# One hand-written instruction order replaced by another in a fused attention and mixture-of-experts kernel

## The chip, the cores and the metric

The kernel runs on one core of one Trainium2 chip. The metric is the device time of one execution in microseconds (us). The engines of the core are named as the profile names them: PE (TensorE matmuls) and PEld (its weight loads), DVE (VectorE), ACT (ScalarE), POOL (GpSimd, which here also issues the casting loads) and SP (SyncE, which issues the other transfers). Every engine works through its own instructions in the order in which the program has them, and waits on semaphores for the others.

## What is computed

Linear attention with phi(x) = elu(x) + 1 over 8 batches, 8 heads, 576 positions and 64 channels; its output, 4608 tokens of width 512, goes into a mixture of 8 experts whose gates are balanced by eight Sinkhorn rounds.

```python
q_p, k_p = (phi(q), phi(k))
kv = np.einsum('bhsd,bhse->bhde', k_p, v)
z = np.sum(k_p, axis=2)
num = np.einsum('bhsd,bhde->bhse', q_p, kv)
den = np.einsum('bhsd,bhd->bhs', q_p, z)[..., None] + 1e-06
x = (num / den)                     # as 4608 x 512
P = np.exp(x @ w_gate - max)        # 4608 x 8
for _ in range(8):
    P /= P.sum(1, keepdims=True) + 1e-09
    P /= P.sum(0, keepdims=True) + 1e-09
    P *= N / E
for e in range(E):
    out += P[:, e:e + 1] * (np.maximum(x @ w1[e], 0.0) @ w2[e])
```

## The kernel before

**Stages.** Attention runs over 16 pairs of heads (`att`, numbered 0 to 15 below as pair n). Of each pair, K, Q and V are loaded; ACT takes an exponential of K and of Q (`f_e`, `f_qe`); DVE makes phi from them (`f_t` and `f_m` for K, `f_qm` and `f_qp` for Q); PE forms the key-value product (`f_kv`, line 411) and transposes phi(Q) (`f_qt`, line 437); copies out of PSUM follow (`f_z` twice, `f_qc`); then PE makes the denominators (`f_den`), ACT their logarithm and reciprocal (`f_ln`, `f_ex`), PE the numerators (`f_num`, line 468), and DVE the quotient into xT (`f_x`, line 496). K of pair 0 is loaded through SP, all the other K, Q, V and all weights through POOL, with a cast on the way for Q, V and the weights; at most eight of POOL's loads are outstanding (`p_sw`). Before there is real work, PE runs up to 46 idle matmuls on a block of zeros (`f_warm`, line 588), which the order places one by one.

The experts run over 9 groups of 512 tokens. Expert 0 begins while attention still runs: a group's first layer (`f_hq`, line 682, and its relu `f_rl`, lines 687 and 689) and second layer (`f_y`, line 930, and its eviction `f_fin`) need only the tokens of that group. From the fifth group on, both layers use a fast matrix scheme with seven products in place of eight (`block7` for the first layer with its products in line 808, `unit` for the second with line 1048). One expert and one group make a unit, numbered 9e + g; from unit 9 on, the repeating pattern, every unit has the same work and its PE order is a fixed chain. A unit needs sums of its hidden layer (`f_S`, line 1019, four a unit). An expert needs, once, four combinations W of its first weights (`f_W`, line 980) and four combinations T of its second weights (`f_T`, line 994), each one DVE instruction with both inputs in SBUF. Results are evicted with their gate into `acc`: most by DVE (line 1079), two a unit by an ACT multiplication (line 1086) and a POOL addition (line 1089). What expert 0 left in `acc` before the gates were known is scaled later, 32 instructions named `f_s`, by ACT or DVE.

**What sets the order.** The class `_Plan` holds 4744 tasks, each with an id, the engines that can do it, a duration, and what it depends on. `run` emits them one at a time. First it takes the tasks of `_FRONT`, a list of ids written out by hand, each with a letter for the engine: p PE, a ACT, d DVE, g POOL, s SP, m a transfer, n nothing. After the list has ended, a greedy rule chooses: the engine that can start earliest, and of its tasks the one of the lowest `prio`. Only the order on each engine, and for tasks that two engines can do the choice of engine, reach the program. The list of before has 1510 entries. It ends in unit 17, the last of expert 1.

Ids that matter below: pair 0 has 50 (load Q), 52 (load V), 54 (`f_e`), 55 (`f_t`), 56 (`f_m`), 58 (`f_kv`), 59 and 60 (`f_z`), 62 to 64 (`f_qe`, `f_qm`, `f_qp`), 65 (`f_qt`), 66 (`f_qc`), 67 (`f_den`); 76 and 78 load K and Q of pair 1, 82 is its `f_e`; 109, 111, 114 and 116 load the quarters of expert 0's first weights; 533 closes the attention; 1535 and 1537 load the first weights of expert 2 and 1541 the second; 1544 to 1547 are the four `f_W` of expert 2, 1548 to 1551 its four `f_T`. An `f_T` may not start before a product of an earlier unit is done, which for 1551 is in unit 17:

```python
tT = add(("dve", 0.685), f_T, deps=tw2 + ([x_closed[0]] if e > 0 else xu[0] + xu[1]) + [tT, pe_id.get((NG * (e - 1) + i + 5, "b22"))], acq=[gT] if i == 0 and e > 0 else [], use=[gw2, gT],
         prio=-900.0 if e > 1 else 5.0)
```

Of the kernel before, what the change touches and what calls it, by code (L numbers as in the profile page):

```python
# [17 lines left out]
class _Plan:  # L18
# [121 lines left out]
    1n 108n 119n 607n 48s 49m 2p 3p 52g 53m 4p 50g 51m 5p 6p 76g 77m 7p 8p 0g 9p 78g 79m 10p 54a 55d 11p 126g 127m  # L140
    12p 13p 14p 15p 80g 81m 16p 56d 17p 18p 128g 129m 19p 20p 21p 57n 22p 130g 131m 23p 24p 25p 154g 155m 26p 27p 28p
    29p 30p 31p 61n 32p 62a 63d 33p 34p 35p 36p 58p 64d 156g 157m 82a 109g 110m 37p 59d 65p 60d 89n 111g 112m 38p 90a
    66d 39p 83d 67p 40p 158g 159m 68a 41p 84d 42p 43p 132a 44p 133d 69p 85n 114g 115m 86p 91d 70a 92d 87a 71a 116g
    117m 139n 93p 141d 45p 94d 88a 140a 182g 183m 72p 46p 73d 95p 96a 134d 74p 184g 185m 160a 97p 75d 135n 142d 98a
    136p 167n 186g 187m 161d 143p 137a 99a 138d 47p 120g 121m 144d 100p 101d 145p 113n 210g 211m 608p 146a 162d 102p
    609p 168a 103d 610p 163n 212g 213m 147p 169d 164p 148a 170d 149a 214g 215m 171p 165d 611p 166d 172a 150p 118n
    240g 241m 612p 151d 614p 613a 616p 615a 152p 242g 243m 618p 153d 173p 620p 189d 123g 124m 195n 188a 174a 622p
    190d 196a 197d 175p 191n 244g 245m 192p 621a 198d 176a 623d 624p 193a 619a 194d 199p 617d 625a 626p 122n 268g
    269m 177a 200d 180p 644n 201p 630p 181d 202a 217d 178p 628p 179d 223n 216a 224a 203p 298g 299m 627d 645p 218d
    270g 271m 204a 647p 225d 219n 205a 226d 328g 329m 220p 646d 106g 107m 648a 227p 247d 221a 649p 222a 228d 253n  # L150
    246a 206p 650d 229p 651p 254a 255d 207d 653p 230a 300g 301m 248d 125n 208p 654a 231p 104g 105m 209d 629p 232a
    256d 249n 272g 273m 233a 250p 636d 652d 257p 251a 252a 631p 275d 258d 632p 305d 259p 236p 638d 655p 281n 274a
    304a 260a 276d 282a 633p 237d 261p 283d 234p 262a 634p 284d 384g 385m 235d 263a 302g 303m 285p 311n 657p 326g
    327m 286d 339n 312a 354g 355m 266p 341d 238p 267d 340a 330g 331m 277n 306d 278p 239a 656a 356g 357m 640d 635p
    279a 342d 358g 359m 280a 658a 313d 287p 264p 314d 288a 659p 307n 265d 642a 289p 677n 290a 308p 333d 332a 660d
    315p 386g 387m 309d 678p 291a 316d 382g 383m 680p 310d 412g 413m 361d 360a 317p 292p 663p 318a 293d 440g 441m
    367n 679a 334d 319p 414g 415m 294p 320a 665p 295d 335n 681a 343p 362d 321a 336p 344d 395n 368a 397d 296p 337d
    369d 338a 568d 666p 297a 396a 389d 322p 345p 323d 682p 442g 443m 346a 370d 673a 324p 416g 417m 684p 325d 363n
    388a 347p 398d 364p 348a 499g 500m 683d 349a 371p 365d 472g 473m 569d 686p 372d 470g 471m 366a 685a 352p 373p
    353d 661p 374a 390d 418a 425n 350p 375p 351d 688p 391n 376a 687d 392p 419d 377a 399p 420d 468g 469m 393a 690p  # L160
    400d 444g 445m 394a 446a 453n 380p 455d 401p 381d 662p 402a 570d 378p 426a 664p 379d 421n 403p 689a 427d 422p
    428d 404a 501g 502m 477s 447d 691a 478s 429p 503g 504m 479s 423a 671d 692p 405a 508s 430d 667p 454a 424d 448d
    431p 406p 432a 668p 407d 669a 433p 509s 516n 456d 710n 408p 434a 711p 409d 449n 693a 457p 675d 510s 511g 435a
    571s 572m 589d 450p 573s 574m 505a 484n 590d 696p 458d 518d 451a 697p 517a 452d 486d 459p 591d 436p 460a 694p
    592s 593m 437d 704a 461p 506d 438p 462a 695p 439d 712a 410p 507d 463a 519d 512n 464p 713p 411a 485a 465d 520p
    475d 466p 521a 700p 467d 715p 487d 702a 474a 561d 488p 562d 513p 714a 476d 701p 489d 514a 480n 515a 563d 522p
    716d 564s 565m 481p 523a 566s 567m 524p 482d 717p 525a 483d 575d 527p 526a 490p 698p 576d 718a 528d 719p 491a
    529p 492p 530d 721p 493a 582d 720a 497p 699p 494a 583d 722d 723p 706a 498d 725p 724a 747d 708a 495p 584d 751n
    752p 726a 496d 585s 586m 587s 588m 754p 748d 559n 577d 531p 790d 755a 578s 579m 580s 581m 848d 727p 532a 753a
    533n 743d 728p 534d 594s 595m 756p 733p 757a 744d 734p 849d 745d 535p 758p 741a 536d 760p 537d 759a 762p 761a  # L170
    764p 763a 735a 766p 791d 596g 765a 597n 603n 792d 746d 729p 793s 794m 850d 560p 749d 851s 852m 730p 853s 854m
    750d 538p 798p 737a 539d 731p 795s 796m 799a 540d 767a 732p 1021s 1022m 804p 1078s 1079m 739a 797n 802p 805a 772p
    803a 768d 812p 769d 773a 808p 813a 770d 541p 800p 774p 771d 801a 542d 818p 809d 814p 819a 543d 778p 815a 776p
    806p 777a 816p 779d 822p 817a 820p 823d 810p 807d 782p 811a 821d 775a 544p 824p 545d 856p 825a 906d 858p 857a
    783d 780p 859a 907d 784p 826d 827d 862p 785a 855n 860p 908d 863a 781d 864p 909s 910m 830p 911s 912m 604g 605m
    598g 599m 600g 601m 546d 832p 831a 861a 870p 836p 871a 865d 876p 837d 872p 877a 547p 874p 828d 873a 880p 548d
    875a 866p 881d 833a 878p 829d 840p 867d 882p 841d 868p 834p 879d 869a 549d 883a 914p 842p 915a 835a 838p 606n
    843a 920p 913n 884d 550p 928p 921a 885d 916p 888p 551d 917a 964d 918p 889a 965d 922p 919a 839d 924p 894p 886d
    929a 923d 890p 602n 925d 930p 887d 934p 931a 966d 932p 895d 935a 967s 968m 926p 969s 970m 552d 933a 892p 927a
    936p 891a 972p 938p 973a 898p 939d 978p 899d 553p 940p 937d 900p 941a 554d 555d 896p 901a 979a 976p 971n 974p  # L180
    982p 975a 986p 977a 980p 942d 946p 987a 893d 983d 992p 990p 943d 993a 988p 947a 897d 996p 989a 984p 944d 952p
    985a 1013d 950p 1014d 953a 991a 1015d 994p 948p 981d 997d 956p 949a 945d 1024p 1016d 954p 1025a 957d 998p 958p
    999a 1534n 1535g 1536m 1026p 1537g 1538m 959a 1012n 1023n 1017d 1030p 1027a 995d 1000p 1031a 955d 556p 1032p 557d
    1001p 558d 1028p 703a 846d 1034p 639d 1002p 1008a 738d 1029a 1035d 1003p 670a 1033d 1036p 1018d 1038p 643d 1004p
    1039a 787d 951a 709d 1040p 1539n 740d 1037a 1044p 1009d 1041a 1005p 674d 1045a 676d 1046p 847a 637d 1042p 904a
    1019d 1006p 1043a 788d 1048p 705d 1081p 1047d 1007p 1049d 1082a 641d 1083p 1080n 1540n 1010d 1050p 1084a 1087p
    1020d 1135s 1136m 1541g 1542m 1051a 1089p 1011d 1088a 1085p 1052d 1056p 1086a 1053d 1058p 1057a 1054d 1061p 1055d
    1059d 1091p 1062a 1060d 1066p 1064a 1063g 1090d 960a 1069p 1092d 672a 1067d 707a 1093p 1068d 1095p 1071d 1097p
    1070d 1096a 1072p 1098a 1094a 1101p 1543n 1074d 1103p 1073d 1102a 1099p 1104d 1105p 1100a 1138p 1106d 1140p 1139a
    1075p 1141a 742a 1107p 1077d 1137n 1144p 1076d 1108a 1192s 1193m 1146p 1109d 1142p 1113p 1110d 1115p 1111d 1114a  # L190
    905d 1145a 1118p 1112d 1116d 1148p 1121a 1117d 1123p 789a 1149d 1122g 1143a 1126p 1065g 1124d 1147d 1150p 1125d
    1152p 1151a 1128d 1154p 1153a 1129p 1155a 1158p 1130d 1160p 1131d 1159a 1156p 1162p 1157a 1195p 1163d 1119a 1197p
    1196a 1120g 962d 1132p 1198a 1161d 1164p 1133d 1194n 1201p 1134d 1165a 1249s 1250m 1203p 844d 736a 1199p 1166d
    1170p 1202a 1127d 1167d 1172p 1171a 1168d 1200a 1175p 1173d 1169d 1205p 1178a 1174d 1180p 1176a 1206d 1183p 1204d
    1181d 1207p 1182d 1209p 1185d 1211p 1210a 1186p 1212a 1208a 1215p 1187d 1217p 1184d 1216a 1213p 1188d 1219p 1214a
    1252p 1220d 1254p 1253a 1218d 1189p 1255a 1221p 1191d 1251n 1258p 1190d 1222a 1306s 1307m 1260p 786a 1223d 1256p
    1227p 1259a 1224d 1257a 1229p 1225d 1228a 1226d 1232p 1261d 1262p 1230d 1233a 1237p 1231d 1234g 1263d 1240p 1179g
# [1009 lines left out]
```

## Time and profile before

| | |
|---|---|
| median of 3 runs | 963.76 us (963.01 to 964.25) |
| the profiled execution | 965.29 us |
| its span, first to last instruction | 963.5 us |
| ACT busy | 579.6 us (60%) |
| POOL busy | 146.1 us (15%) |
| DMA, mean | 117 GB/s |
| granted TensorE clock, mean | 1.000 |

Times inside the profile count from the start of the span; 1.8 us of the profiled execution lie outside it. A table by windows gives, for every stretch, the busy time of each engine with the number of its instructions in brackets. In a timeline each line has the start, the duration, the engine and the instruction, and in square brackets how long the engine had been idle before it and who released it.

### The profile page before, as it was taken

How to read it: one execution, taken by the hardware profiler on the slowest of the kernel's cores; microseconds unless marked ns; L12 is line 12 of the kernel's file. 1: busy time of each engine (PE TensorE's matmuls, PEld its weight loads, DVE VectorE, ACT ScalarE, POOL GpSimd, SP SyncE). 2: the span in 40 equal slices, each digit the busy share in tenths (PEclk: the TensorE clock that was granted, in tenths of full speed). 3: DMA queues.
4: the chain of work that ended last, by engine and by line, in shares of the span. 5: the costliest groups of instructions: out<-in, count | busy, mean ns of one | idle time of the engine just before them, and what ended most of it. 6: DMA issues, size and time to landing. Idle time of an engine off the chain costs nothing.

```text
span 963.5 us, 21102 instructions
## 1 busy us (share of the span) xinstructions
PE 950.4 (99%) x8576; PEld 804.8 (84%) x8576; DVE 784.7 (81%) x1501; ACT 579.6 (60%) x1032; POOL 146.1 (15%) x210
## 2 busy tenths in 40 slices
PE   8999999999999999999999999999999999999998
PEld 4555578788888888888888888888888888888886
DVE  6999999987788888878887888878887888877775
ACT  6999765666655555555555555555555555555552
POOL 6442000010112111111111111111112111111110
PEclk9999999999999999999999999999999999999999
DMA  9998391252227222362227222272226322235654
GB/s 227 267 235 202 136 252 67 44 122 78 78 78 165 78 77 78 101 142 77 78 78 157 86 78 78 73 163 69 70 73 138 97 75 76 78 100 164 165 162 112
DMA packets 45693, 112.52 MB, mean 117 GB/s; under 512 B 4380, under 2 KB 25628, under 8 KB 45596
## 3 DMA queue, kind: packets, MB, share of 16 engines
q1 hardware_dynamic: 21068, 75.57, 23.4%
q0 software_dynamic: 24128, 35.07, 19.2%
q8 instruction: 67, 1.10, 0.4%
q10 hardware_dynamic: 400, 0.52, 0.2%
q14 instruction: 30, 0.25, 0.1%
HBM read 119.69 MB, written 17.69 MB: 143 GB/s over the span
## 4 chain that ended last, share of the span: by engine, by line
PE 89%; DVE 4%; DMA 3%; ACT 2%; issue 1%; SPq 1%; POOL 0%; DVEq 0%; POOLq 0%; ACTq 0%
PE ye L1048 35%; PE hq L808 23%; PE R L808 12%; PE Zye L1048 6%; PE Zye L808 6%; PE ye L930 2%; PE hq L682 2%; DMA xs<-xd 2%; DMA kin<-in_k_dram 1%; PE yw L588 1%; DVE xT L496 1%; PE kv_ps L411 1%; PE att L468 0%; PE num_ps L468 0%; ACT rden L481 0%
## 5 line engine op out<-in xcount | busy, mean ns | idle before, releaser
L1079 DVE SCALAR_TENSOR_TENSOR acc<-ye,P_sb,acc 128x256 f32<-128x256 f32 x620 | 268.1, 479 | 124.5 <-PE ye L1048 123.1
L808 PEld LDWEIGHTS <-W 128*128 128x128 f16 x2144 | 209.8, 98 | 25.3
L1048 PEld LDWEIGHTS <-S 128*128 128x128 f16 x1984 | 194.1, 98 | 23.8 <-DVE S L1019 1.0
L1048 PE MATMUL ye<-T,S 128*128 128x256 f16 x1488 | 192.8, 273 | 0.9 <-DVE S L1019 0.8
L1089 POOL TENSOR_TENSOR acc<-acc,st 128x256 f32<-128x256 f32 x124 | 87.8, 727 | 626.2 <-ACT st L1086 626.2
L808 PEld LDWEIGHTS <-w 128*128 128x128 f16 x1608 | 157.4, 98 | 19.1 <-issue 0.5
L1048 PEld LDWEIGHTS <-h 128*128 128x128 f16 x1584 | 154.9, 98 | 19.4 <-issue 1.4
L843 ACT ACTIVATE h<-hq 128x512 f16<-128x512 f32 x134 | 80.0, 598 | 148.5 <-PE hq L808 145.7
L808 PE MATMUL hq<-xs,W 128*128 128x256 f16 x1008 | 151.2, 273 | 0.0
L808 PE MATMUL R<-xs,W 128*128 128x256 f16 x1008 | 151.2, 273 | 0.0
L808 PE MATMUL hq<-xs,w 128*128 128x256 f16 x1008 | 140.9, 273 | 0.3 <-DVE h L846 0.3
L840 ACT ACTIVATE h<-Zye 128x512 f16<-128x512 f32 x134 | 80.2, 598 | 39.2 <-PE Zye L808 39.2
L1086 ACT ACTIVATE st<-Zye,P_sb 128x256 f32<-128x256 f32 x124 | 52.5, 471 | 76.3 <-PE Zye L1048 75.5
L846 DVE CUSTOM_DVE_ANT_0 h<-R,s 128x512 f16<-128x512 f32 x126 | 86.5, 687 | 9.9 <-ACT s L830 9.9
L1019 DVE TENSOR_TENSOR S<-h 128x1024 f16<-128x1024 f16 x124 | 85.3, 688 | 11.0 <-ACT h L843 11.0
L830 ACT COPY s<-hq 128x512 f32<-128x512 f32 x126 | 73.5, 584 | 34.3 <-PE hq L808 34.2
L823 ACT COPY Zye<-hq 128x512 f32<-128x512 f32 x134 | 77.8, 580 | 21.8 <-PE hq L808 21.7
L846 DVE CUSTOM_DVE_ANT_0 h<-hq,s 128x512 f16<-128x512 f32 x126 | 86.6, 688 | 4.7 <-PE hq L808 4.5
L808 PE MATMUL Zye<-xs,w 128*128 128x256 f16 x504 | 75.6, 273 | 0.0
L837 ACT COPY s<-R 128x512 f32<-128x512 f32 x126 | 74.5, 591 | 0.7 <-PE R L808 0.7
L1048 PE MATMUL ye<-w,h 128*128 128x256 f16 x528 | 68.4, 273 | 1.2 <-DVE acc L1079 1.2
L1048 PE MATMUL Zye<-w,h 128*128 128x256 f16 x528 | 68.4, 273 | 0.0
(117 smaller groups left out, 979.2 us busy)
## 6 DMA issues: line engine op xcount, KB each, us to landing
xs<-xd SPq DMA_DIRECT2D x63, 896.0 KB, 4.5
kin<-in_k_dram POOLq DMA_DIRECT2D x15, 576.0 KB, 8.6
out_dram<-acc SPq DMA_DIRECT2D x67, 128.0 KB, 2.4
w<-in_moe_w_dram POOLq DMA_DIRECT2D x16, 512.0 KB, 9.5
w<-in_moe_w_dram POOLq DMA_DIRECT2D x7, 1024.0 KB, 13.1
vv<-in_v_dram POOLq DMA_DIRECT2D x16, 288.0 KB, 7.6
qin<-in_q_dram POOLq DMA_DIRECT2D x16, 288.0 KB, 9.0
xd<-acc SPq DMA_DIRECT2D x5, 512.0 KB, 2.7
```

The costliest lines, as they stand in the source:

```text
L808: nc.tensor.matmul(dst[:, p, :], lhsT=lhs(p, c), rhs=rhs(c), start=(first and p == 0 and c == 0), stop=(c == 1), skip_group_check=True)
L823: nc.scalar.copy(out=Zt[1], in_=gX["tile"])
L830: nc.scalar.copy(out=gs2["tile"], in_=gX["tile"])
L837: nc.scalar.copy(out=gs5["tile"], in_=gR["tile"])
L840: nc.scalar.activation(out=hd(0, 0), in_=Zt[1], func=AF.Relu)
L843: nc.scalar.activation(out=hd(1, 0), in_=gX["tile"], func=AF.Relu)
L846: nc.vector._custom_dve(TENSOR_ADD_SAT, out=dst, in0=ps, in1=sb, s0=3.0e38, s1=0.0)
L1019: nc.vector.tensor_tensor(out=Sx[:, i], in0=a0, in1=a1, op=op)
L1048: nc.tensor.matmul(bank(g_)[:, s, :], lhsT=lhs(s, kk), rhs=rhs(kk), start=(new and s == 0 and kk == 0), stop=(kk == 3), skip_group_check=True)
L1079: nc.vector.scalar_tensor_tensor(out=dst(), in0=bank(g_)[:, s, :], scalar=P_sb[:, gg, e:e + 1], in1=dst(), op0=ALU.mult, op1=ALU.add)
L1086: nc.scalar.mul(out=gst["tile"], in_=bank(g_)[:, s, :], mul=P_sb[:, gg, e:e + 1])
L1089: nc.gpsimd.tensor_tensor(out=dst(), in0=dst(), in1=gst["tile"], op=ALU.add)
```

## The change

Only the text of `_FRONT` changes. The tasks, their dependencies and the greedy rule are the same. The new list has 1518 entries: the same 1510 tasks and eight more, all of units 16 and 17 and of expert 2's combinations (1548, 1549, 1550, 1463, 1464, 1469, 1470, 1499). 55 tasks that either engine can do change theirs, 29 from DVE to ACT and 26 from ACT to DVE. The PE order differs up to its 339th of 503 entries, which is in unit 10, and is the same from there. Its core, in which "..." stands for what is left out:

```diff
 _FRONT = """
-    1n 108n 119n 607n 48s 49m 2p 3p 52g 53m 4p 50g 51m 5p 6p 76g 77m 7p 8p 0g 9p 78g 79m 10p 54a 55d 11p 126g 127m
-    12p 13p 14p 15p 80g 81m 16p 56d 17p 18p 128g 129m 19p 20p 21p 57n 22p 130g 131m 23p 24p 25p 154g 155m 26p 27p 28p
-    29p 30p 31p 61n 32p 62a 63d 33p 34p 35p 36p 58p 64d 156g 157m 82a 109g 110m 37p 59d 65p 60d 89n 111g 112m 38p 90a
...
-    1465p 1489d 1491d 1468p 1467d 1466d 1492p 1544d 1494p 1493a 1496p 1545d 1495a 1471p 1497a 1546d 1500p 1547d 1502p
-    1501a 1472d 1498p 1473d 1504p
+    1n 108n 119n 607n 48s 49m 2p 3p 50g 51m 4p 52g 53m 5p 6p 0g 7p 8p 76g 77m 9p 78g 79m 10p 54a 55d 11p 80g 81m 12p
+    13p 14p 15p 126g 127m 16p 17p 18p 109g 110m 19p 20p 21p 61n 62a 63d 22p 128g 129m 23p 24p 25p 130g 131m 26p 27p
+    64d 28p 29p 30p 56d 31p 111g 112m 65p 57n 58p 66d 154g 155m 32p 59a 33p 82a 34p 60d 35p 67p 36p 89n 156g 157m 91d
...
+    1173d 786a 1174d 1205p 1200a 1169d 1180p 902a 1206d 1176a 1183p 1181d 1177g 1182d 1207p 1185d 1209p 1184d 1211p
+    1544d 1210a 1186p 1212a 1545d 1208a 1215p 788d 1217p 1204d 1216a 1213p 1187d 1178a 1219p 1188d 1214a 1179g 1252p
...
+    1291g 1297p 1236g 1296d 1546d 1321p 1295d 1323p 1322a 1299d 1325p 1298d 1324a 1300p 1318d 1326a 1329p 1543n 1301d
+    1331p 1547d 1330a 1327p 1302d 1333p 1328a 1332d 1366p 1292a 1368p 1334d 1367a 1303p 1369a 1335p 1304d 1365n 1372p
...
+    1402d 1397d 1433p 1404a 1408p 1401d 1405g 1434d 1411p 1410d 1548d 1435p 1409d 1437p 1436a 1413d 1439p 1412d 1438a
+    1414p 961d 1440a 1549d 1443p 1416d 1445p 1444a 1415d 1441p 1447p 1442a 1480p 1448d 1482p 1481a 1417p 1483a 1449p
...
+    1485a 1460p 1454d 1458d 1490p 1463a 1459d 1465p 1464g 1491d 1468p 1466d 1467d 1492p 1489d 1494p 1550d 1496p 1495a
+    1471p 1470d 1497a 1469d 1493a 1500p 1473d 1502p 1472d 1501a 1498p 1504p 1499a
 """
```

## The prediction

> **What bounds the kernel now.** I read the engines' shares first, then the table by windows of 25 us, then the timeline wherever a window was not full.
>
> ```profile
> PE 950.4 (99%) x8576; PEld 804.8 (84%) x8576; DVE 784.7 (81%) x1501; ACT 579.6 (60%) x1032; POOL 146.1 (15%) x210
> ...
> PE   8999999999999999999999999999999999999998
> ```
>
> PE sets the time. An order of the same matmuls can save only what PE spends idle, or on idle matmuls of zeros.
>
> ```profile
> 0.00:25.00 25.00, 20.38 (x143) 10.31 (x144) 15.90 (x28) 15.06 (x17) 15.99 (x28) 1.00 1.04 226
> 25.00:50.00 25.00, 24.69 (x208) 14.02 (x206) 22.82 (x37) 24.24 (x33) 10.55 (x15) 1.00 1.17 264
> 50.00:75.00 25.00, 23.76 (x265) 14.72 (x263) 23.17 (x40) 23.66 (x33) 11.19 (x15) 1.00 1.03 235
> ...
> 250.00:275.00 25.00, 25.00 (x231) 22.40 (x230) 19.72 (x39) 15.05 (x30) 4.97 (x7) 1.00 0.20 74
> 275.00:300.00 25.00, 22.99 (x210) 20.19 (x209) 23.06 (x44) 12.46 (x25) 5.19 (x7) 1.00 0.45 117
> 300.00:325.00 25.00, 25.00 (x232) 22.40 (x230) 19.23 (x37) 14.43 (x28) 2.82 (x4) 1.00 0.49 117
> ```
>
> The columns after the length are PE, PEld, DVE, ACT and POOL busy, each with its instructions in brackets, then granted clock, DMA share and GB/s. Two places are not full. In the first 75 us PE lacks 4.6, 0.3 and 1.2 us, and ACT and DVE are nearly full from 25 us on: attention is held by these two. Then 275 to 300 lacks 2.0 us, and has 210 matmuls where its neighbours have 231 and 232. At 25/231 = 0.108 us each that is 21 x 0.108 = 2.3 us; I use this figure, since the modelled ends of matmuls cover part of a gap. Here DVE is busy 23.06 us against 19.72 before it.
>
> ```profile
> 287.48 0.68 DVE L994 TENSOR_TENSOR T<-w 128x1024 f16<-128x1024 f16 x1
> ...
> 288.82 1.16 DVE L994 TENSOR_TENSOR T<-w,T 128x1024 f16<-128x1024 f16 x1
> ...
> 290.30 0.68 DVE L994 TENSOR_TENSOR T<-w 128x1024 f16<-128x1024 f16 x1
> ...
> 291.29 0.68 DVE L994 TENSOR_TENSOR T<-w,T 128x1024 f16<-128x1024 f16 x1
> ...
> 291.89 0.86 DVE L1079 SCALAR_TENSOR_TENSOR acc<-ye,P_sb,acc 128x256 f32<-128x256 f32 x2
> 292.67 1.27 DVE L846 CUSTOM_DVE_ANT_0 h<-R,s 128x512 f16<-128x512 f32 x2
> 292.80 1.03 PE L1048 MATMUL ye<-w,h 128*128 128x256 f16 x8 [1.24 <-DVE acc L1079]
> ```
>
> The list of before ends here. It put all four W of expert 2 (1544 to 1547) at its very end, and the greedy rule added all four T straight after them. Eight instructions of 0.68 us reach DVE within 9 us, the evictions of 291.89 come late, and PE waits for them, then 0.8 us more for the sums S behind them.
>
> **The change, part by part.** (1) The combinations of expert 2. I placed each list entry by the PE entry ahead of it and took that matmul's time in this trace. W moves from 284-286 us to 224, 224, 246 and 250; T stands at 271, 273 and 284; only 1551 is left to the greedy rule, behind unit 17's product as its dependency asks. No instruction is added. The stall goes: -2.3 us. What hides the seven moved ones is DVE's idle time: 19.6 to 19.9 us busy of 25 in the three windows from 200 to 275, so 2.5 us idle in a unit of 12.2 us. 7 x 0.68 = 4.8 us is spread over five units. The nearest rows are those of later experts, where W and T come one a unit: from 300 to 925 us every window has PE at 25.00. If that cover were gone the cost would be the whole 4.8 us. I take 0.
>
> The second T above took 1.16 us, 0.48 more than the others; it began while POOL was still adding (two additions, 287.83 to 289.42). The Trainium skill (SBUF — State Buffer, the section on the ports) says that VectorE and GpSimd share a port pair under an exclusive lock, which a VectorE instruction with two SBUF inputs wants too when the GpSimd one reads SBUF, and the later one blocks. The trace agrees with that row; by the rule a spread-out W or T could meet one of a unit's two additions, at 0.48 us each; the sum would stay, since DVE's idle time covers that too, but rival (B) below would cost 7 x 0.48 = 3.4 us more, 969.6.
>
> The weights must be there. 1535 and 1537 move from PE time 177 to 187 and 1541 from 192 to 241; medians from issue to landing are 9.5 and 13.1 us, so they land near 197 and 254, ahead of 224 and 271 by 27 and 17 us. Nothing.
>
> (2) The start. POOL now issues Q of pair 0 ahead of V. Issued at 1.66, V took 5.1 us to land (6.8 us); Q, issued at 2.51, took 7.2 (9.7), and ACT began at once:
>
> ```profile
> 9.78 1.16 ACT L445 ACTIVATE eq<-qin 128x1152 f16<-128x1152 f16 x1 [4.01 <-DMA qin<-in_q_dram]
> ...
> 10.98 0.76 DVE L452 TENSOR_TENSOR tq<-tq,eq 128x1152 f16<-128x1152 f16 x1 [0.73 <-ACT eq L445]
> 11.27 1.16 ACT L382 ACTIVATE ek<-kin 128x1152 f16<-128x1152 f32 x1 [0.32 <-DMA kin<-in_k_dram]
> 11.95 0.69 PEld L411 LDWEIGHTS <-t 64*128 64x128 f16 x18 [0.42 <-DVE tq L452]
> ...
> 14.68 0.40 PE L468 MATMUL att<-qpT,kvz 128*128 128x288 f16 x2 [0.56 <-DVE qpT L333]
> ```
>
> With the two landings exchanged: exponential 6.8 to 7.9, phi(Q) by 8.7, K's minimum by 9.5. PE now has 30 idle matmuls ahead, not 35 (14 at 0.43 us apart, 16 at 0.21: until 10.7). Transpose 10.7 to 11.3, key-value product to 12.2, copies to 12.75, first denominators at 12.8 against 14.68: 1.9 us earlier. But one copy (59) is now on ACT, ahead of pair 1's exponential (82), which therefore begins at 12.6, not 11.27. The same ACT steps, added on: the reciprocal of pair 0 ends at 17.7 (before 18.86), but pair 2's exponential, done at 16.9 before, ends at 19.6. At 19.3 us ACT has done as much as before; DVE is some 0.8 us ahead. Bounds 0 and 1.9.
>
> (3) The rest of attention. I summed what each list has given ACT and DVE at the entry where 92 us of useful PE work are listed, each instruction at its row's mean (exponential 1.16, logarithm 0.74, relu 0.59 or 0.69, quotient 0.76): ACT 107.0 before and 105.0 after, DVE 107.2 both times. ACT, 24.2 of 25 us busy, is the tighter of the two, so the same PE work is ready up to 2.0 us earlier. I take half, as DVE gives nothing, and count (2) within it, since a lead on DVE alone is used up by ACT: together -1.2. Bounds: -3.9 (both in full) and, as a new order can open new waits, +2.5 (priced below).
>
> (4) The middle. Between 105 and 155 us of PE work DVE gets 0.9 us more than before. DVE is idle 25 - 23.05 plus 25 - 24.05 = 2.9 us from 125 to 175, so this costs 0, and 0.9 without that cover. The Sinkhorn rounds end at 155.6 us of PE work against 156.9, and the `f_s` scales move into units 10 to 15, whose DVE slack is that of (1). Nothing.
>
> **Sum.** -2.3 - 1.2 = -3.5. The profiled execution was 965.29, its span 963.5 with 1.8 around it; both fall by 3.5. It lies 1.53 above the median of the runs, so for the median 963.76 - 3.5 = 960.3.
>
> **Rivals.** (A) The front gives the gain back. POOL's queue now has two weight quarters (109, 111) ahead of K of pair 3. Two quarters in a row landed at 22.65 and 23.92 in the trace, 1.27 us apart, so this K lands near 20.7 + 2 x 1.27 = 23.2. For it: before, its exponential began at 21.1, 0.4 us after landing. Against: the new list has it two ACT instructions later, near 23.8. If the 2.5 us reach PE: 963.76 - 2.3 + 2.5 = 964.0.
>
> (B) Slower: the moved W and T land ahead of something that PE waits for. All seven exposed cost 4.8 against the 2.3 saved: 963.76 + 2.5 = 966.2 with the front at nothing. It decides from 0.33 us exposed on each (2.3/7). For it: 1544 and 1545 share one unit with three scales, ahead of a relu (1204) that a product waits for. Against: the later experts' rows.
>
> (C) The start counts in full and ACT's lead too: 963.76 - 2.3 - 3.9 = 957.6. For it: ACT is full from 25 us. Against: DVE is too, and its list is not shorter.
>
> (D) The change doesn't do what it says: the T still come in one heap, because 1541 is issued late or 1551 waits. Then only the front is left: 963.76 - 1.2 = 962.6. Against: the 17 us above.
>
> **How the numbers follow.** Forecast 0.62, (C) 0.13, (A) 0.10, (B) 0.08, (D) 0.07. The range leaves out the far ends of (A), (B) and (C): 957.8 to 963.6. A measurement of this kernel tells about 0.2%, 1.9 us, from no change: below 961.8 is faster. Of the forecast's own 0.62 some 0.08 lie above that, since without the 1.2 us of the front 961.5 is left; with (C) that makes 0.54 + 0.13 + 0.08 from the lower parts of (A) and (D) = 0.75 faster. Slower is (B) and a tail of (A): 0.09. The rest, 0.16, is no change.
>
> **What would show it.** Right: 275 to 300 us has about 231 matmuls and PE 25.00, no PE wait for line 1079 over 0.5 us near 290, W and T one at a time from about 222; first denominators near 12.8 us. Wrong: PE waits for DVE between 200 and 290 us (B), or windows from 25 to 125 us emptier than before with waits for kin (A). The prediction fails if the front moves by more than 2 us either way.

## The result, and the profile after

| | before | after |
|---|---|---|
| median of 7 runs each, on the same chip | 964.25 us (963.01 to 966.12) | 961.01 us (960.58 to 963.27) |
| ratio | | 0.9967 [0.9954, 0.998] |
| the profiled execution, its span | 965.29, 963.5 us | 963.27, 961.5 us |

That is 3.2 us less; 3.5 were forecast. But the profiled execution of after is the slowest of its seven, and it will turn out that it lost at the start what most executions do not lose. Its engines' shares, from the page, and its table by windows (columns as before: length, PE, PEld, DVE, ACT, POOL busy with instructions in brackets, granted clock, DMA share, GB/s):

```profile
PE 950.4 (99%) x8576; PEld 805.4 (84%) x8576; DVE 783.0 (81%) x1498; ACT 580.1 (60%) x1035; POOL 146.0 (15%) x210
```

```profile
0.00:25.00 25.00, 20.51 (x142) 10.38 (x143) 14.79 (x26) 15.02 (x18) 15.61 (x27) 0.95 1.03 217
25.00:50.00 25.00, 24.17 (x204) 13.69 (x202) 22.18 (x36) 22.44 (x31) 10.78 (x15) 0.99 1.17 248
50.00:75.00 25.00, 24.59 (x266) 15.03 (x263) 23.68 (x39) 24.36 (x35) 10.62 (x14) 1.00 1.00 240
...
225.00:250.00 25.00, 25.00 (x231) 22.40 (x230) 21.73 (x43) 16.28 (x31) 3.74 (x5) 1.00 0.50 117
250.00:275.00 25.00, 25.00 (x231) 22.32 (x230) 20.93 (x41) 14.89 (x29) 3.00 (x4) 1.00 0.21 74
275.00:300.00 25.00, 25.00 (x232) 22.40 (x230) 20.81 (x41) 14.51 (x28) 6.44 (x8) 1.00 0.45 118
```

The window from 275 to 300 us now has 232 matmuls and PE at 25.00, against 210 and 22.99. DVE, which had 23.06 us there, has 20.81; what left it shows in the window from 225 to 250, 21.73 against 19.55, and does no harm to PE. The first two windows are another matter: the clock was not granted in full (0.95 and 0.99, against 1.00), and there are no more matmuls in them than before.

The moved instructions in the timeline of after:

```profile
224.18 0.68 DVE L980 TENSOR_TENSOR W<-w 128x1024 f16<-128x1024 f16 x1
...
224.90 0.69 DVE L980 TENSOR_TENSOR W<-W,w 128x1024 f16<-128x1024 f16 x1
...
247.33 0.82 DVE L980 TENSOR_TENSOR W<-w 128x1024 f16<-128x1024 f16 x1
...
250.32 0.68 DVE L980 TENSOR_TENSOR W<-w,W 128x1024 f16<-128x1024 f16 x1
...
272.03 0.68 DVE L994 TENSOR_TENSOR T<-w 128x1024 f16<-128x1024 f16 x1
...
274.20 0.68 DVE L994 TENSOR_TENSOR T<-w,T 128x1024 f16<-128x1024 f16 x1
...
285.21 0.67 DVE L994 TENSOR_TENSOR T<-w 128x1024 f16<-128x1024 f16 x1
...
289.00 0.68 DVE L994 TENSOR_TENSOR T<-w,T 128x1024 f16<-128x1024 f16 x1
289.06 1.21 POOL L1089 TENSOR_TENSOR acc<-acc,st 128x256 f32<-128x256 f32 x1 [5.42 <-ACT st L1086]
```

The W and T come one or two at a time over 65 us, and from 205 to 300 us the view of waits has no wait of PE at all.

To compare lists I read from each trace when the matmul behind the first k began, the 46 idle ones of line 588 left out. Between the 2200th and the 2600th lies the place of the old heap; with no stall this takes 43.72 us. All moments in us from the start of the span:

| trace | clock released | first denominators | key-value product of pair 2 | 1000th matmul | 2200th | 2600th | 2200 to 2600, over 43.72 |
|---|---|---|---|---|---|---|---|
| before | 7.36 | 14.68 | 21.96 | 127.76 | 262.80 | 308.80 | 2.28 |
| x1 | 6.07 | 14.04 | 21.32 | 126.43 | 261.05 | 304.82 | 0.05 |
| x3 | 5.04 | 13.54 | 20.94 | 126.47 | 261.36 | 306.71 | 1.63 |
| after | 5.22 | 12.48 | 21.64 | 128.73 | 263.03 | 306.75 | 0.00 |
| x0 (new list again) | 5.77 | 12.49 | 19.91 | 125.86 | 260.17 | 303.89 | 0.00 |
| x4 | 6.72 | 12.96 | 20.38 | 126.37 | 260.68 | 304.40 | 0.00 |
| x2 | 6.11 | 12.66 | 22.55 | 129.07 | 263.38 | 309.92 | 2.82 |
| x9 | 5.51 | 12.36 | 21.86 | 129.18 | 263.49 | 307.21 | 0.00 |

The column "clock released" needs a word. In every trace the idle matmuls follow one another every 0.43 us at first and every 0.22 us later: PE's clock starts at half and is granted in full from a moment that differs from execution to execution, 4.6 to 7.4 us in these traces. (The clock in the tables by windows leaves this first stretch out.) The idle matmuls are counted, not timed, so a late release delays what stands behind them: with the list of before the first key-value product began at 11.95, 11.32 and 10.81 us for releases at 7.36, 6.07 and 5.04, 0.5 us for each us. Two starts are compared only after this is taken off. Further on the correction is rough: x1 and x3 have the same front, and at equal release x3 reaches the 2200th matmul 0.8 us later.

The last column settles the heap: 2.28 us before, nothing after. But the profiled execution of after reaches the 2200th matmul at 263.03, no earlier than before, whereas x0, the same list, reaches it at 260.17. The timeline of after's start shows where they part:

```profile
7.90 1.16 ACT L445 ACTIVATE eq<-qin 128x1152 f16<-128x1152 f16 x1 [2.13 <-DMA qin<-in_q_dram]
...
9.91 0.68 PE L437 MATMUL att<-ident,tq 128*128 128x128 f16 x9
...
10.58 0.92 PE L411 MATMUL kv_ps<-vv,t 64*128 64x192 f16 x18
...
12.48 0.42 PE L468 MATMUL att<-qpT,kvz 128*128 128x288 f16 x2
...
20.75 0.76 DVE L452 TENSOR_TENSOR tq<-tq,eq 128x1152 f16<-128x1152 f16 x1
...
21.64 1.05 PE L411 MATMUL kv_ps<-vv,t 64*128 64x192 f16 x18 [1.67 <-DVE tq L452]
22.04 0.72 POOL L372 DMA_DIRECT2D qin<-in_q_dram  x1 [1.76 <-DMA vv<-in_v_dram]
```

The first denominators came at 12.48, where 12.8 was forecast, but partly by luck: Q landed at 7.88 and not at 6.8, and the clock was released 2.1 us earlier than in before. Then PE stood 1.67 us ahead of the key-value product of pair 2. The view names DVE's phi(Q), which ended at 21.51, but POOL waited for a V in the same stretch; V of pair 2 landed at 21.50, so both fit (x4 below decides for V). In x0 this V landed at 19.75 and nothing waited for it. What came of the gap, in windows cut at multiples of 3.41 us from the release of the clock, again in after:

```profile
15.46:18.87 3.41, 2.48 (x18) 1.39 (x19) 2.17 (x5) 2.98 (x5) 1.21 (x2) 1.00 1.23 204
18.87:22.29 3.42, 1.55 (x21) 0.97 (x21) 2.53 (x5) 2.33 (x3) 0.98 (x2) 1.00 1.11 253
22.29:25.70 3.41, 3.41 (x24) 1.99 (x19) 2.11 (x4) 2.90 (x4) 1.95 (x3) 0.50 1.18 215
```

After a window with PE busy for 1.55 of 3.42 us, the granted clock fell to 0.50 for one such window. The gap and the half clock together are why the 1000th matmul came at 128.73 instead of about 126.

### The profile page after: what moved, and what is told of

It is laid out like the page before. It is cut to its first block, busy times and chain, and to the rows that moved or that the text cites. A ratio compares the mean times of both kernels' runs of the same rounds, so it can differ in the third digit from the quotient of the medians.

```text
span 961.5 us, 21100 instructions
## 1 busy us (share of the span) xinstructions
PE 950.4 (99%) x8576; PEld 805.4 (84%) x8576; DVE 783.0 (81%) x1498; ACT 580.1 (60%) x1035; POOL 146.0 (15%) x210
## 4 chain that ended last, share of the span: by engine, by line
PE 93%; ACT 2%; DMA 2%; DVE 2%; issue 1%; POOL 0%; DVEq 0%; POOLq 0%
PE ye L1048 36%; PE hq L808 24%; PE R L808 12%; PE Zye L808 6%; PE Zye L1048 6%; PE ye L930 3%; PE hq L682 2%; DMA kin<-in_k_dram 1%; PE kv_ps L411 1%; PE att L437 1%; DMA vv<-in_v_dram 1%; PE num_ps L468 1%; PE att L468 1%; ACT rden L481 0%; DVE xT L496 0%
```

## The experiments

Each ran beside the list of before on the same chip; x1 to x4 on one chip, x0, x5, x6 and x8 on a second, x9 to x12 on a third. "Expected" is what was written ahead of the run. In the diffs only ids of the list are shown; "@ 1211p" gives the entry behind which a line goes.

### x1: the seven combinations alone, in the list of before

```diff
-    1544d ... 1545d ... 1546d ... 1547d      (unit 17)
+    @ 1211p  1544d      @ 1186p  1545d      @ 1296d  1546d      @ 1331p  1547d
+    @ 1410d  1548d      @ 1414p  1549d      @ 1494p  1550d
```

> The list of before with only the seven combinations of expert 2 (four W, three T) put where the new list has them. Theory, the heap of eight combinations on DVE is what cost PE 2.3 us, and spreading them costs nothing: 964.25 - 2.3 = 962.0 us, ratio to before 0.9976, about 231 matmuls from 275 to 300 us. Rival, the gain of the new list comes from its front and the wait only moves: 964.2, ratio 1.000, PE waits for DVE somewhere between 220 and 290 us.

961.91 us (960.98 to 962.66, 11 runs) against 963.76 (27 runs), 0.998 [0.9971, 0.9989]. The windows of x1 at the old heap's place and ahead of it, and one T in its timeline:

```profile
250.00:275.00 25.00, 25.00 (x230) 22.32 (x229) 20.79 (x40) 14.68 (x29) 4.97 (x7) 1.00 0.22 74
275.00:300.00 25.00, 25.00 (x231) 22.40 (x230) 20.58 (x41) 14.22 (x28) 5.03 (x7) 1.00 0.54 128
```

```profile
269.01 1.41 POOL L1089 TENSOR_TENSOR acc<-acc,st 128x256 f32<-128x256 f32 x2 [5.72 <-ACT st L1086]
...
269.80 1.17 DVE L994 TENSOR_TENSOR T<-w 128x1024 f16<-128x1024 f16 x1
```

The stall is gone with the old front. One T met the additions of POOL and took 1.17 us, the case priced at 0.48 in the prediction, and PE stayed at 25.00 all the same: DVE's idle time covers that too. By the medians the heap was worth 1.9 us, by the trace 2.23; the interval, 1.1 to 2.8 us, holds both.

### x2: the seven back in unit 17, the rest of the new list kept

```diff
-    1544d to 1550d      (where the new list has them)
+    @ 1492p  1544d      @ 1496p  1545d      @ 1471p  1546d      @ 1500p  1547d
```

> The new list with the seven combinations put back to the end, where before has them. Theory: the stall at 290 us is back, 961.0 + 2.3 = 963.3 us, ratio to before 0.999; what is left of the gain is the front's, near 1 us. Rival, the front brought the gain: 961.0, ratio 0.997.

964.6 us (962.67 to 966.76, 11 runs), 1.0006 [0.9995, 1.0016]. The heap is back; the window of x2 there:

```profile
275.00:300.00 25.00, 23.00 (x206) 19.67 (x204) 22.82 (x43) 12.47 (x24) 5.04 (x7) 1.00 0.41 108
```

It costs 2.82 us here, 0.5 more than in before. The new front should have shown alone, as a gain, and did not. In its trace V of pair 2 was late again: PE idle for 2.50 us ahead of the product at 22.55, then the half clock from 23.18 for 3.41 us. With the larger stall 963.8 would be expected in place of 963.3; the late V explains the other 0.8 us only in part, since 2 of the 11 executions have the lower mean clock that goes with such a fall (0.998 or less), and the other nine have a median of 964.0. Taken alone, x2 would put the front between 1.0 us gained and 1.0 lost.

### x3: only the four W moved, in the list of before

```diff
-    1544d ... 1545d ... 1546d ... 1547d      (unit 17)
+    @ 1211p  1544d      @ 1186p  1545d      @ 1296d  1546d      @ 1331p  1547d
```

> The list of before with only the four W moved; the four T still come in one heap of 4 x 0.68 = 2.7 us where the list ends. Theory, DVE's idle time of a unit (2.5 us) hides what fits into it: 0.2 us of stall is left, 962.1 us, ratio 0.998. Rival, each late combination is exposed by the same share (2.3 / 8 = 0.29 us): half of the stall is left, 963.1, ratio 0.999. A third way, the T are the harmful ones since they come last: all 2.3 us stay, ratio 1.000.

963.6 us (962.75 to 964.32, 11 runs), 0.9999 [0.999, 1.0008]: no gain that can be told. The trace says why. PE's waits in x3 between 284 and 296 us:

```profile
PE ye L1048 <- DVE S L1019: 0.8, 1, 0.8
PE ye L1048 <- DVE acc L1079: 0.5, 1, 0.5
```

Columns: who waited for whom, us in total, times, longest. The four T alone, which the greedy rule adds in a row, leave 1.63 of the 2.28 us; the 0.65 us that are gone lie inside the interval, which allows a gain of up to 1.0. None of the three expectations holds cleanly: half the heap leaves neither a tenth of the stall nor half of it nor all.

### x8: the four W in one heap elsewhere, in the new list

```diff
-    1544d, 1545d, 1546d      (at three places)
+    @ 1331p  1544d 1545d 1546d 1547d
```

> The new list with the four W of expert 2 in one heap in unit 14 (after PE entry 1331) in place of four places; the T stay spread. Theory, a heap of 2.7 us costs what exceeds DVE's slack at that place, and a heap of four T cost 1.6 us by its trace: PE waits 0.5 to 1.6 us near 250 us, 961.5 to 962.6. Rival, only the T are harmful, because they come in the last unit of an expert: no wait, 961.0.

962.57 us (961.95 to 963.04, 11 runs), 0.9984 [0.9975, 0.9993], against 960.7 for the same list without the heap (x0, same chip): 1.9 us worse. From x8's timeline:

```profile
247.86 0.68 DVE L980 TENSOR_TENSOR W<-w 128x1024 f16<-128x1024 f16 x1
...
248.58 0.69 DVE L980 TENSOR_TENSOR W<-W,w 128x1024 f16<-128x1024 f16 x1
...
249.19 0.69 DVE L980 TENSOR_TENSOR W<-w 128x1024 f16<-128x1024 f16 x1
...
249.79 0.68 DVE L980 TENSOR_TENSOR W<-w,W 128x1024 f16<-128x1024 f16 x1
...
250.39 0.48 DVE L1079 SCALAR_TENSOR_TENSOR acc<-ye,P_sb,acc 128x256 f32<-128x256 f32 x1
...
250.92 1.03 PE L1048 MATMUL ye<-T,h 128*128 128x256 f16 x8 [0.88 <-DVE acc L1079]
```

The eviction stands behind four combinations and PE stands for it, 40 us away from the old place and with the same instructions that cost nothing when spread. The stretch from the 1400th to the 2200th matmul takes 92.03 us against 90.67 in x0, 1.4 more. So it is the heap, not the place at the list's end and not the work.

### x4: one weight quarter behind V of pair 2, in the new list

```diff
-    18p 109g 110m
+    130g 131m 109g 110m
```

> The new list with one load in POOL's queue moved: the first quarter of expert 0's weights goes behind Q and V of pair 2, where the new list had it ahead of them. Theory, the new start is 2 us ahead until V of pair 2 lands at 21.5 us, late by one transfer behind the quarter, and PE's clock drops in the gap: V lands near 20, the key-value product of pair 2 starts 1.5 us earlier, the clock does not drop, and 0.5 to 1.5 us are gained: 959.5 to 960.5 us, ratio to before 0.995 to 0.996. Rival, ACT and DVE are full from there and use the lead up in any case: 961.0, ratio 0.997.

960.68 us (959.89 to 960.89, 5 runs), 0.9968 [0.9955, 0.998], on the chip where x2 had 964.6. V landed at 18.23; the product of pair 2 in x4's timeline:

```profile
20.38 0.92 PE L411 MATMUL kv_ps<-vv,t 64*128 64x192 f16 x18 [0.30 <-DVE xT L496]
...
20.80 0.76 DVE L452 TENSOR_TENSOR tq<-tq,eq 128x1152 f16<-128x1152 f16 x1
```

It begins ahead of the phi(Q) that the view had named as its releaser in after, so that instruction is no part of what it needs: in after it was V. Of the 3.9 us between x2 and x4 the heap explains 2.8; 1.1 are left, of which the late V is a part, not shown to be all.

### x0: the new list once more

> The changed kernel itself beside the three kernels that differ from it by one edit each, on the same chip. 961.0 us, ratio to before 0.997; in its profile PE waits about 1.8 us for V of pair 2 near 20 us.

960.7 us (960.38 to 961.12, 5 runs), 0.9968 [0.9955, 0.998]. V landed at 19.75, the product began at 19.91, and the clock did not fall. The wait that was expected is thus not a property of the list; it comes in some executions. With V on time x4's edit changes nothing that five executions of each can tell (0.9968 both times).

### x9: both quarters ahead of Q and V of pair 2

```diff
-    18p 109g 110m 19p ... 31p 111g 112m 65p
+    18p 109g 110m 111g 112m 19p ... 31p 65p
```

> The new list with a second weight quarter ahead of Q and V of pair 2 in POOL's queue, so that V lands one transfer (1.2 us) later than it otherwise would. Theory, the late V alone makes the gap, and the gap the drop of the clock: V lands at 21 to 22.5 us, the key-value product of pair 2 starts right behind it, the clock drops to one half for 3.4 us in most executions, and the time is 2 to 3 us over the new list's 960.7: 962.7 to 963.7, ratio to before 0.999 to 1.000. Rival, ACT and DVE set the pace and a later V is hidden: 960.7 to 961.2, ratio 0.997.

961.98 us (961.08 to 964.76, 11 runs), 0.9979 [0.997, 0.9988]. V landed at 21.72, and now the view names it. PE's waits in x9 between 19 and 24 us:

```profile
PE kv_ps L411 <- DMA vv<-in_v_dram: 1.7, 1, 1.7
```

How often this happens can be counted over all timed executions: one stretch of 3.41 us at half clock takes 3.41 x 0.5 / 961 = 0.0018 off the mean granted clock. A mean of 0.998 or less was seen in 7 of 11 executions of x9 (two quarters ahead), at a median of 962.5 us, where the other four took 961.1 to 961.4. With one quarter ahead it was 1 of 12 for the new list, 2 of 11 for x2, 3 of 11 for x10 and none of 32 for x5, x6 and x8; with none ahead, none of 10 (x4 and x12). It is not the new list's own: before had it in 7 of 80, at 965.6 to 966.5 us against a median near 964. So two quarters ahead make it frequent; one quarter, 6 of 66, cannot be told from before. The time, 961.98, is between the expected 962.7 to 963.7 and the rival's 960.7 to 961.2, as 4 of the 11 executions escape.

### x6: V of pair 0 ahead of Q again, in the new list

```diff
-    50g 51m 4p 52g 53m
+    52g 53m 50g 51m 4p
```

> The new list with V of pair 0 loaded ahead of Q again, as before has it; all else as in the new list. Theory, the start's lead is used up by the wait for V of pair 2 at 21.5 us, so losing it costs nothing: first denominators near 14.3 us in place of 12.5, time as the new list, 961.0. Rival, the lead reaches the end: 1.5 to 1.9 us more, 962.5 to 962.9.

961.76 us (961.0 to 962.27, 10 runs), 0.9976 [0.9967, 0.9985], 1.1 us over x0 on the same chip. Its trace shows less: Q landed at 8.51 (7.37 in x0), the first denominators came at 13.11 for a release at 6.26, which is 0.37 us behind x0 at equal release. In x0 phi(Q) was ready at 9.35, and behind the idle matmuls the transpose began at 9.99: these, not Q, held the transpose for the last 0.6 us. The 14.3 us that were expected for the denominators did not come. So the exchange is worth some 0.4 us at the start; whether 0.4 or 1.1 us of it reach the end, two intervals that overlap and one trace do not settle.

### x10, x11, x12: fewer idle matmuls ahead of the first work

x10 has 26 instead of 30 ahead of the new list's first transpose, x11 has 30 instead of 35 ahead of the first key-value product of before, x12 is x10 with x4's quarter. The ones taken out stand further back, so that each list keeps its 46. For x11:

```diff
-    32p 33p 34p 35p 36p      (ahead of 58p)
+    @ 58p  three of them      @ 65p  two of them
```

> The new list with 26 idle matmuls ahead of the first transpose in place of 30; the four stand later, two behind the first key-value product, one ahead of pair 0's numerators, one ahead of pair 2's key-value product. Theory, PE's queue of idle matmuls and not the landing of Q sets the start: the first transpose starts 0.6 us earlier (when phi(Q) is ready), first denominators 0.5 us earlier at the same moment of the clock's release, and 0.2 to 0.5 us reach the end: 960.3, ratio 0.9965. Rival, ACT and DVE use it up: 960.7, ratio 0.997.

> The list of before with 30 idle matmuls ahead of its first key-value product in place of 35; the five stand right behind it and behind the first transpose. Q still lands after V. Theory, the idle matmuls set much of the difference between the two starts: first denominators 0.6 us earlier than before at the same moment of the clock's release, 0.3 to 0.6 us reach the end, 963.3 to 963.6, ratio 0.9995. Rival, the landing of Q does: nothing moves, ratio 1.000.

> The new list with the weight quarter behind V of pair 2 and with the four idle matmuls moved, the two edits that looked good or harmless alone. Expected 960.0 to 960.6, ratio 0.996 to 0.9968, no drop of the clock in any execution; if neither edit reaches the end, 960.7.

x10: 961.52 us (959.97 to 963.7, 11 runs), 0.9976 [0.9967, 0.9985]. x11: 963.41 (962.74 to 966.09, 11), 0.9998 [0.9989, 1.0007]. x12: 960.59 (960.13 to 961.12, 5), 0.9963 [0.9949, 0.9977]. In x10 the transpose began at 9.32 and the denominators at 12.14: 0.3 us ahead of x0 and level with it at equal release, where 0.6 and 0.5 were expected; in its trace V of pair 2 was late, and the clock fell. In x11 the first key-value product began at 9.51 and the denominators at 12.74, 1.1 and 0.6 us ahead of x3 once the releases (4.59 and 5.04) are made equal. The ratio did not move, but its interval allows a gain of 1.1 us, so whether such a lead is lost later is not shown. x12 has the lowest ratio of all, but it cannot be told from x4 and x0.

### x5: six idle matmuls just ahead of the product of pair 2, in the new list

```diff
-    46p      (its old place)
+    97p 46p      (where 46 now issues six idle matmuls)
```

> The new list with one idle matmul task moved ahead of the key-value product of pair 2 and made six matmuls of zeros long (1.3 us of PE time), so that PE has work in the gap in which it waits for V of pair 2; nothing else moves. Theory, the drop of the granted clock to one half for 3.4 us after the gap costs time of its own: the clock stays at 1.00, 0.5 to 1.0 us less than the new list, 960.0 to 960.5. Rival, the drop is harmless because ACT and DVE set the time there: the same as the new list, 961.0.

961.51 us (960.53 to 962.58, 11 runs), 0.9972 [0.9963, 0.9981], 0.8 over x0. V was on time in its trace, and the idle matmuls only stood in the way: the product began at 21.26 for a release at 6.63, against 20.38 for 6.72 in x4. In this trace they cost 0.9 us with nothing to guard against. None of the 11 executions has the lower mean clock, but the new list without them has it in 1 of 12 only, so whether they would keep the clock up is not shown.

## Why the prediction was right, and where it was not

**The heap, -2.3.** Right in size and in reason. The trace gives 2.28, x1 removes it alone, x2 brings it back, x8 makes another of the same instructions. The price of the moved seven, 0, is right too: PE at 25.00 from 200 to 300 us. What was not foreseen is how the stall divides: the four T alone make 1.6 us (x3), four W alone 1.4 (x8), and all eight 2.3 to 2.8.

The prediction weighed a rule of the Trainium skill (SBUF — State Buffer, "SBUF: two separate sides"): of a VectorE instruction with two SBUF inputs and a GpSimd one that reads SBUF, the later one blocks. The rows agree on both sides. In after the T of 289.00 began 0.06 us ahead of a POOL addition and kept its 0.68 us, and the addition took 1.21 instead of 0.73; in x1 the T of 269.80 came second and took 1.17.

**The start, -1.9, counted within the front.** The first denominators came at 12.48, but for a release at 5.22 instead of 7.36. At equal release (x4 at 6.72, 12.96; 0.3 us added for 7.36) they come near 13.3, 1.4 us ahead of before. The forecast had 1.9, with Q landing at 6.8 us where 7.4 and 7.9 were seen. The exchanged landings carry 0.37 of the 1.4 in x6's trace and five fewer idle matmuls 0.6 in x11's; the remaining 0.4 may be the transpose ahead of the product, which no run tried. Not to add the lead to the rest fits the total; x11 alone does not show that such a lead brings nothing.

**The rest of attention, -1.2.** About right in size where V is on time, and in part for another reason. x0 and x4 lie 1.2 us (0.0012 in the ratio) below x1, which has the heap's gain alone; the intervals overlap, but all five executions of x4 are below all eleven of x1 on the same chip. The traces agree: at a release of 6.07 the 2200th matmul comes at 261.05 to 262.2 in the four with the old front (x1, x11, x3, before) and near 260.3 in x0 and x4, 0.7 to 1.8 us apart. But 0.33 us of this is won behind attention (below, the middle). That ACT's shorter list is the cause of the rest was argued, and no run tried it; when the 600th and the 800th matmul begin, ACT has indeed been busy 1.0 and 0.7 us less in x0 than in before. What the order of Q and V has in it (x6, 0.4 to 1.1 us) is not settled.

**Rival (A), the weight quarters.** It was given a chance of 0.10 for K of pair 3. K of pair 3 landed at 23.89 in after, its exponential began at 24.06, and PE had no wait for it. The mechanism is real, but the load was V of pair 2, and the prediction had no line for it. Where it strikes it costs 1 to 3 us, with 2.5 set for it: in x9 the executions with the fall lie 1.3 us above the others, the profiled execution of after took 963.27 us where the other six have a median of 961.0, and its 2200th matmul is 3.1 us behind x0's at equal release (263.03, against 260.17 less 0.3), since the gap also brings 3.41 us of half clock. It struck in 1 of 12 executions of the new list, which is why the median does not show it; x9 shows what it does to a median where V is often late.

**(B), (C), (D).** Not so: no moved instruction is waited for (B), the front gave about 1 us and not 3.9 (C), the T come apart (D).

**The middle, 0.** Here the forecast left out a small gain. From the 1400th to the 2200th matmul, some 172 to 263 us, PE takes 91.0 us in all four traces with the old front, and 90.67 in each of the nine with the new one that have no heap there. In before one wait of PE stands in this stretch, 0.17 us by the view, behind two of the scales `f_s` that DVE has at 215.13 and 217.40:

```profile
217.40 0.47 DVE L898 TENSOR_SCALAR acc<-acc,P_sb 128x512 f32<-128x512 f32 x1
...
218.91 1.03 PE L1048 MATMUL ye<-T,S 128*128 128x256 f16 x8 [0.17 <-DVE acc L1079]
```

With the new front this wait is gone; in x0 the scales of these microseconds are on ACT. The prediction had the scales move and put the whole middle at nothing. That they made the wait is likely, and no run tried it.

## What to carry to other kernels

Look at what stands at the end of a list written by hand and at what a rule adds behind it: eight small instructions in one heap cost 2.3 us of the bounding engine, and nothing one by one in the same engine's idle time. When a load is moved ahead of others on a queue, follow the ones behind it until each is needed, and judge by how often they come late over many executions, not by one trace. Compare the start of two traces only after their clock release is made equal.

## What the runs showed of the hardware

The granted clock fell to 0.50 for 3.41 us in after, x2, x9 and x10, each time five stretches of 3.41 us after its release. Cut from the release into such stretches, the table by windows has PE busy for 1.55, 0.92, 1.53 and 1.80 us in the one ahead of the fall. In the other ten traces the emptiest stretch of the first 40 us has 1.94 us (x8) to 2.58 (x5), and the clock stayed; it also stayed after 1.93 us in before's heap (from 290.67). So in these traces, if the busy time of this view is what counts, the limit lies between 1.80 and 1.93 us of 3.41, a little over half. The Trainium skill (TensorE: Matmul & The Clock Gate, "What's actually happening") has the clock fall after at least one idle window of some 3.4 us; by these rows the window need not be idle.

Of a T or W on DVE and an addition on POOL that overlap, the later one loses a little less than the time for which the earlier one still runs: for 0.61 to 0.63 us it lost 0.48; for 0.27 (after, the W of 247.33) and 0.33 (before, the addition behind the T of 287.48), 0.14 and 0.18; for 0.12 (x1, the T of 287.49), nothing.

The same load of the same list landed at 19.75 us in one execution and at 21.50 in another.
